# Attention into two MoE blocks: the third turning moved to a scores' bank, and a row tile's scaling moved behind the minimum passes

## The chip, the cores and the metric

The kernel runs on one core of a Trainium2 chip. The metric is the time of one execution on the device, in microseconds, as the median of repeated runs; lower is better.

## The reference

Three layers follow each other. S is 576 keys, D is 64, there are 4 batches of 8 heads, so 2304 tokens of 512 numbers behind attention.

```python
scores = scale * np.matmul(q, k.transpose(0, 1, 3, 2))
thresh = np.max(scores, axis=-1, keepdims=True) - tau
scores = np.where(scores >= thresh, scores, -1000000000.0)
attn = np.exp(scores - np.max(scores, axis=-1, keepdims=True))
attn = attn / (np.sum(attn, axis=-1, keepdims=True) + 1e-09)
x = np.matmul(attn, v)                      # turned to [2304, 512]
...
noisy_logits = x @ w_gate + np.log1p(np.exp(x @ w_noise)) * noise
top2 = np.argpartition(-noisy_logits, 2, axis=1)[:, :2]
...
h = np.maximum(x[mask] @ w1[e], 0.0)        # for each of 8 experts, 512 -> 1024
out[mask] += top2_w[mask, k, None] * (h @ w2[e])
...
h = x @ w_in                                # 512 -> 2048
out = (np.maximum(h, 0.0) + alpha * np.minimum(h, 0.0)) @ w_out
```

## The kernel before

**Precision.** Every large matmul is done as three products of split operands: a high part, cast by ScalarE, and a low part, which POOL or VectorE makes as the difference of the number and its high part. L306 and L308 cast the high parts of q and k (`split_hi`), L316 on POOL makes the low parts (`split_lo`); L171 and L177 do the same for expert weights (`w_hi`, `w_lo`), L206 and L207 for expert rows.

**Units of attention.** Attention is cut in 80 units (`NU`): a batch, a block of 128 queries and a pair of heads; the last 64 queries of a batch make a tail unit ("t") that holds both heads in one block. Four units give one tile of 128 tokens. A unit passes these stages, each in an iteration of its own of the loop at L737:

- `s_mm` (L364): 12 matmuls make the scores, one allocation of `psum_s` per head. There are two such allocations, of two banks each; of a bank's 512 columns 288 are used.
- `d1` (L375, VectorE): a pass over the scores of one head that copies them out and finds the row's extreme value; it frees the banks. Called the minimum pass here, since the sign is turned.
- `a1` (L386, ScalarE): the exponential. `thresh` (L380, ScalarE): the threshold.
- `d2` (L399, VectorE): masks the exponentials below the threshold and sums them, called the masking pass.
- `t_mm` (L416, L418, L420, TensorE): turns the masked probabilities by 128x128 blocks, in parts of 4, 4 and 1 blocks, called the first, second and third turning, each into a bank of `psum_t`, of which there are three. `a2` (L428, L430, L432, ScalarE) copies each part out.
- `pv` (L449 to L454): the products with V, in the one allocation of `psum_v`; `group_evac` (L470, L475, L477, ScalarE) copies a finished tile out.

Iteration i works on unit i+1's scores, unit i's minimum, exponential and threshold, unit i-1's masking, unit i-2's turnings (`DT` = 2) and unit i-3's products.

**Stages of a tile.** When a tile is out, `x_stages` spreads its later steps over the next iterations: `rows` (L488 and L489 invert the sums; L498 turns the tile, L500 on VectorE scales it, L502 stores it), `logits` (L508, copied by L511 on ScalarE), `flip` (L515 turns the logits), `sum_` (L519, L522 on VectorE). `gating` then computes noisy logits, top-2 (L570 to L577, VectorE), ranks (L582 to L587, TensorE), places (L593 to L597) and sends the rows to the experts' lists (L617, L618, POOL) for groups of three tiles.

**What sets the order.** The order is written by hand: on each engine instructions run in the order in which the program issues them, and buffers are handed out in rings. A table `at` holds extra steps by iteration and slot; before, slot 0 lies behind the next unit's scores and ahead of `pv`, slot 1 at the iteration's end. An instruction that uses a PSUM bank waits for whoever used that bank before it.

**Expert 0.** Its first 256 rows don't depend on gating's result. From iteration 66 on its weights are loaded and split, in iterations 78 and 79 its two row tiles are turned (L203 in `x_split`, in a `psum_t` bank) and split, and from iteration 80 on `do_fill` puts one piece of its products (L214 first, then L232) into each iteration. Behind the loop the other experts and the last layer follow.

## Time and profile before

| | us |
|---|---|
| median of 3 runs | 1167.44 |
| lowest and highest run | 1166.29, 1167.62 |
| the profiled execution's own time | 1170.81 |
| its span | 1169.1 |

| engine | busy us | share of the span |
|---|---|---|
| TensorE, matmuls (PE) | 1135.2 | 97% |
| TensorE, weight loads (PEld) | 977.5 | 84% |
| VectorE (DVE) | 622.8 | 53% |
| ScalarE (ACT) | 532.0 | 46% |
| GpSimd (POOL) | 532.8 | 46% |

The mean granted clock of TensorE is 0.997 of full speed. A row of the timeline gives start and length in us, engine, line, operation and tiles, how many instructions it joins and, in brackets, how long the engine was idle ahead of it and whose end it waited for. Attention runs from the start to about 320 us, the experts and the last layer fill the rest.

### The profile page before, as it was taken

What the parts mean: (1) busy time and instruction counts of PE and PEld (TensorE: products, weight loads), DVE (VectorE), ACT (ScalarE), POOL (GpSimd) and SP (SyncE); (2) the same over time, 40 slices, a digit from 0 to 9 for tenths busy, and PEclk for the clock granted to TensorE, in tenths of its full rate; (3) what the DMA queues carried; (4) which work ended last, traced back from release to release, by engine and by line L of the source; (5) the groups of instructions that cost most, each with busy time, mean ns of one, the idle gap of its engine ahead of it and who ended that gap; (6) DMA issues with size and microseconds to landing.
All of it is one profiled execution on the core that took longest, in us unless ns stands there. A gap on an engine that the chain in (4) does not pass through costs nothing. (4 is left out here: it accounts for less than half of the span.)

```text
span 1169.1 us, 20453 instructions
## 1 busy us (share of the span) xinstructions
PE 1135.2 (97%) x7754; PEld 977.5 (84%) x7754; DVE 622.8 (53%) x1332; ACT 532.0 (46%) x1039; POOL 532.8 (46%) x632
## 2 busy tenths in 40 slices
PE   7999989999899999999999999999999999999997
PEld 6887777877789999999989898998888888888886
DVE  7978788899644544454545453445443343342221
ACT  7977768788624544444444454433211211211111
POOL 7636534654524545455454555556332333332221
PEclk9999999999999999999999999999999999999999
DMA  7423222132357676567667565541321321320001
GB/s 219 137 86 122 92 77 74 73 119 92 136 141 207 184 199 194 183 171 213 192 189 202 186 188 190 166 151 54 86 66 25 92 66 27 90 64 10 36 1 39
DMA packets 156552, 141.50 MB, mean 121 GB/s; under 512 B 108576, under 2 KB 109216, under 8 KB 156448
## 3 DMA queue, kind: packets, MB, share of 16 engines
q1 hardware_dynamic: 150400, 120.91, 35.1%
q0 software_dynamic: 5760, 18.88, 4.8%
q8 instruction: 63, 1.03, 0.4%
q14 instruction: 41, 0.34, 0.1%
q10 hardware_dynamic: 288, 0.34, 0.1%
HBM read 97.11 MB, written 42.99 MB: 120 GB/s over the span
## 5 line engine op out<-in xcount | busy, mean ns | idle before, releaser
L214 PE MATMUL ps_t<-m_v,m_pair 128*128 128x384 f32 (+2 forms) x1216 | 220.0, 317 | 0.3 <-DVE m_v L207 0.3
L177 POOL TENSOR_TENSOR m_pair<-m_v,m_pair 128x512 fp32r<-128x512 f32 x114 | 151.9, 1353 | 130.0 <-ACT m_pair L171 106.7
L214 PEld LDWEIGHTS ps_t<-m_v,m_pair 128*128 128x128 f32 x1216 | 186.8, 190 | 8.1 <-DVE m_v L207 0.5
L232 PE MATMUL ps_s<-m_pair,m_hh 128*128 128x512 f32 x528 | 167.5, 390 | 0.0
L995 DVE TENSOR_SCALAR m_tmp<-ps_t,alpha_t 128x512 f32<-128x512 f32 (+1 forms) x80 | 55.7, 697 | 208.6 <-PE ps_t L214 200.9
L225 DVE SCALAR_TENSOR_TENSOR m_gate<-ps_t,m_hh 128x384 fp32r<-128x384 f32 (+1 forms) x120 | 58.8, 493 | 169.9 <-ACT m_hh L224 169.8
L399 DVE SCALAR_TENSOR_TENSOR m_hh<-m_tmp,sm,m_hh 128x576 f32<-128x576 f32 x144 | 126.1, 908 | 2.4 <-ACT sm L380 2.0
L214 PE MATMUL ps_t<-m_v,m_early 128*128 128x256 f32 (+2 forms) x672 | 127.3, 320 | 0.0
L232 PEld LDWEIGHTS ps_s<-m_pair,m_hh 128*128 128x128 f32 x528 | 99.1, 188 | 20.3
L1000 POOL TENSOR_TENSOR m_v<-m_tmp,m_v 128x512 fp32r<-128x512 f32 x39 | 50.4, 1293 | 139.7 <-ACT m_v L999 139.7
L375 DVE TENSOR_SCALAR_CACHE_REDUCE m_tmp<-ps_s 128x576 f32<-128x576 f32 x144 | 103.6, 752 | 18.5 <-PE ps_s L364 16.0
L386 ACT ACTIVATE m_hh<-m_tmp,sm 128x576 f32<-128x576 f32 x144 | 105.7, 783 | 11.0 <-DVE m_tmp L375 10.9
L214 PEld LDWEIGHTS ps_t<-m_v,m_early 128*128 128x128 f32 x672 | 105.9, 189 | 5.1 <-DVE m_v L207 0.4
L364 PE MATMUL ps_s<-m_pair 64*128 64x288 f32 (+1 forms) x864 | 95.3, 318 | 12.9 <-DVE m_tmp L375 8.3
L999 ACT CAST m_v<-m_tmp 128x512 fp32r<-128x512 f32 x39 | 24.2, 620 | 173.5 <-DVE m_tmp L996 173.5
L232 PE MATMUL ps_s<-m_pair,m_gate 128*128 128x512 f32 x264 | 102.9, 390 | 0.0
L224 ACT ACTIVATE m_hh<-ps_t 128x384 fp32r<-128x384 f32 (+1 forms) x120 | 52.7, 439 | 98.3 <-PE ps_t L214 96.8
L1000 POOL TENSOR_TENSOR m_gate<-m_tmp,m_gate 128x512 fp32r<-128x512 f32 (+1 forms) x41 | 44.1, 1077 | 116.1 <-ACT m_gate L999 109.9
L364 PEld LDWEIGHTS ps_s<-m_pair 64*128 64x128 f32 (+1 forms) x864 | 72.3, 191 | 28.1 <-DVE m_tmp L375 14.3
L1019 PE MATMUL ps_s<-m_pair,m_v 128*128 128x512 f32 x396 | 95.1, 389 | 0.0
L1019 PE MATMUL ps_s<-m_pair,m_gate 128*128 128x512 f32 x360 | 88.3, 391 | 0.0
L1019 PEld LDWEIGHTS ps_s<-m_pair,m_v 128*128 128x128 f32 x396 | 74.3, 188 | 15.4
(229 smaller groups left out, 1982.0 us busy)
## 6 DMA issues: line engine op xcount, KB each, us to landing
m_v<-in_w_dram SPq DMA_DIRECT2D x64, 512.0 KB
yg<-m_tmp SPq DMA_DIRECT2D x40, 256.0 KB
m_tmp<-in_w_in_dram SPq DMA_DIRECT2D x16, 512.0 KB
m_tmp<-in_w_out_dram SPq DMA_DIRECT2D x16, 512.0 KB
m_early<-in_kt_dram SPq DMA_DIRECT2D x15, 320.0 KB
yg<-m_gate SPq DMA_DIRECT2D x18, 256.0 KB
m_rows<-xg SPq DMA_DIRECT2D x72, 64.0 KB
out_dram<-m_tmp SPq DMA_DIRECT2D x18, 256.0 KB
```

The source lines that it names most:

```text
L177: eng.tensor_tensor(WL[n][:, w], raw[:, w], f32(WH[n][:, w]), op=OP.subtract)
L214: pe.matmul(ps[:, :n], w[wc[d]][:, col:col + 128], x[xx][:, d, :n], start=(k == 0), stop=(k == 11))
L224: act.activation(h, ps, AF.Relu)
L225: dve.scalar_tensor_tensor(hs[1][:, f * n:f * n + n], ps, 0.0, f32(h), op0=OP.max, op1=OP.subtract)
L232: pe.matmul(ps, a[:, o:o + 128], ww[w][:, c:c + 512], start=(f == 0 and k == 0), stop=(f == nf - 1 and k == 2))
L364: pe.matmul(u["ps", h][:, x, :288], lhs, kk[r, o:o + 288], start=(k == 0), stop=(k == 2))
L375: dve.tensor_scalar(u["sp"][:, h].rearrange("p (a b) -> p a b", a=2), ps[:, :, :288], -0.125, None, op0=OP.mult, op1=OP.min, accum_out=u[" ...
L386: act.activation(u["em"][:, h], u["sp"][:, h], AF.Exp, bias=u["sm"][:, h:h + 1], scale=-1.0)
L399: dve.scalar_tensor_tensor(u["em"][:, h], u["sp"][:, h], sm[:, 2 + h:3 + h], u["em"][:, h], op0=OP.is_le, op1=OP.mult, accum_out=acc)
L995: dve.tensor_scalar(g, ps, 0.0, alpha_t[:, f:f + 1], op0=OP.min, op1=OP.mult)
L1000: pool.tensor_tensor(h[:, n:2 * n], g, f32(h[:, :n]), op=OP.subtract)
L1019: pe.matmul(ps, h[x][:, t * 128:t * 128 + 128], ww[w][:, c:c + 512], start=(f == 0 and k == 0), stop=(f == 15 and k == 2))
```

## The change

The third turning of a unit no longer takes a bank of `psum_t`. `s_bank` allocates the next unit's score banks ahead of the turnings, and the third turning writes into columns 384 to 511 of the last of these banks, which the scores leave free; only for the last three units it stays in `psum_t`. ScalarE's copy of it comes behind the threshold and behind the scores in program order. A new slot -1 lies behind the exponentials of unit i and ahead of the masking passes of unit i-1; the scaling of a tile (`scale_rows`), the copy and the sum of its logits, top-2 and the places go there, while the matmuls for them stay at an iteration's end. `split_hi` and `w_hi` go from slot 1 to slot 0. Expert 0's two row tiles are turned in iteration 79 into two score allocations, and split in iteration 80 behind the last `w_hi`. Two pieces of its first product share one allocation.

```diff
--- before.py
+++ after.py
@@ -201,6 +201,9 @@
             else:
                 for c in range(HP):
                     pe.transpose(ps[:, c * 128:c * 128 + 128], src[:, c * 128:c * 128 + 128], ident)
+            x_halves(ps, j, x)
+
+        def x_halves(ps, j, x):
             pv_ = ps.rearrange("p (c t) -> p c t", c=HP)
             xh = x[0][:, :, j * 128:j * 128 + 128]
             act.copy(xh, pv_)
@@ -351,8 +354,6 @@
             b, c, hp = units[i]
             qh, ql, kh, kl, zh, zl = sets[b * HP + hp]
             u = st[i]
-            for h in range(nh(i)):
-                u["ps", h] = psum_s()
             q0 = 0 if c == "t" else c * 128 + (64 if b % 2 else 0)
             for x in range(2):
                 for k, (q, z, kk) in enumerate(((qh, zh, kh), (qh, zh, kl), (ql, zl, kh))):
@@ -365,6 +366,10 @@
 
         def nh(i):
             return 1 if units[i][1] == "t" else 2
+
+        def s_bank(i):
+            for h in range(nh(i)):
+                st[i]["ps", h] = psum_s()
 
         def d1(i, h):
             u = st[i]
@@ -408,7 +413,7 @@
             u = st[i]
             em = u["em"]
             emf = em.rearrange("p h s -> p (h s)")
-            ps = psum_t()
+            ps = psum_t() if part < 2 or i + DT + 1 >= NU else st[i + DT + 1]["ps", nh(i + DT + 1) - 1][:, 1, 384:]
             u["pt", part] = ps
             if part < 2:
                 o = part * 640
@@ -488,27 +493,41 @@
                 dve.tensor_scalar(e, e, 1e-9, None, op0=OP.add)
                 dve.reciprocal(e, e)
 
-            def rows():
+            def turn_rows():
                 x = xts[T]
+                g["rows"] = psum_t()
+                for c in range(HP):
+                    pe.transpose(g["rows"][:, c * 128:c * 128 + 128], x[:, c], ident)
+
+            def scale_rows():
                 e = esum[T]
                 if "inverse" not in g:
                     inverse()
-                ps = psum_t()
-                for c in range(HP):
-                    pe.transpose(ps[:, c * 128:c * 128 + 128], x[:, c], ident)
+                ps = g["rows"]
                 xtok[T] = xtok_ring()
                 dve.tensor_tensor(xtok[T].rearrange("p (h d) -> p h d", h=H), ps.rearrange("p (h d) -> p h d", h=H),
                                   e[:, :, None].to_broadcast([128, H, D]), op=OP.mult)
                 sp.dma_start(xd[T * 128:T * 128 + 128], xtok[T])
 
+            def rows():
+                turn_rows()
+                scale_rows()
+
             def logits():
+                logits_mm()
+                logits_copy()
+
+            def logits_mm():
                 x = xts[T]
                 ps = psum_t()
+                g["lp"] = ps
                 for c in range(HP):
                     pe.matmul(ps[c * 32:c * 32 + 32, :128], wcat[:, c], x[:, c], start=True, stop=True,
                               skip_group_check=True)
+
+            def logits_copy():
                 g["lt"] = lt_ring()
-                act.copy(g["lt"], ps[:, :128])
+                act.copy(g["lt"], g["lp"][:, :128])
 
             def flip():
                 g["ps"] = psum_t()
@@ -521,6 +540,9 @@
                                   esum[T][:, :, None].to_broadcast([128, H, 16]), op=OP.mult)
                 dve.tensor_reduce(lg[:, T], t.rearrange("p (h j) -> p j h", h=H), axis=AX.X, op=OP.add)
 
+            if T < NT - 2:
+                return [(0, 1, turn_rows), (1, -1, scale_rows), (1, 1, logits_mm), (2, -1, logits_copy),
+                        (2, 1, flip), (3, -1, sum_)]
             return [(0, 1, rows), (1, 1, logits), (2, 1, flip), (3, 0, sum_), (0, 0, inverse)]
 
         def bc8(ap, n):
@@ -622,12 +644,12 @@
             sends = [(T, k) for T in range(t0, t1) for k in range(2)]
             first = [exp_, one_plus, log_, noisy, top2]
             if 3 < t1 <= 12:
-                plan = [(d, 1, f) for d, f in enumerate(first)] + [(5, 1, rank), (6, 0, place)]
+                plan = [(d, 1, f) for d, f in enumerate(first[:4])] + [(5, -1, top2), (5, 1, rank), (6, -1, place)]
                 if t1 == FIRST:
                     plan.append((9, 0, close))
                 return plan + [(6 + q, 1, lambda a=a: send(*a)) for q, a in enumerate(sends)]
             if t1 <= 15:
-                plan = [(d // 2, 1, f) for d, f in enumerate(first)] + [(4, 1, rank), (5, 0, place)]
+                plan = [(d // 2, 1, f) for d, f in enumerate(first[:4])] + [(3, -1, top2), (4, 1, rank), (5, -1, place)]
                 return plan + [(5 + q // 2, 1, lambda a=a: send(*a)) for q, a in enumerate(sends)]
             if t1 == NT:
 
@@ -683,7 +705,7 @@
             next_load()
 
         for i, n, p, eng in sched:
-            put(i, split_hi, n, p)
+            put((i, 0) if i > 8 else i, split_hi, n, p)
             put(i + 1, do_lo, n, p, eng)
 
         def zero_init(e):
@@ -700,17 +722,28 @@
         put(64, w_load, 1)
         for n in range(W0):
             i = 66 + 2 * n
-            put(i, w_hi, n)
+            put((i, 0), w_hi, n)
             put(i + 1, w_lo, n, pool)
             put(i + 1, w_load, n + 2)
+        x0_bank = {}
+
+        def x0_turn(t):
+            x0_bank[t] = psum_s()[:, 0]
+            src = xrows.pop((0, t))
+            for c in range(HP):
+                pe.transpose(x0_bank[t][:, c * 128:c * 128 + 128], src[:, c * 128:c * 128 + 128], ident)
+
         for t in range(BLOCK0 // 128):
             put(70, x_load, 0, t)
-            put(NU - 4 + DT + t, lambda t: x_split(xrows.pop((0, t)), t, X0, psum_t, False), t)
+            put(NU - 1, x0_turn, t)
+            put((NU, 0), lambda t: x_halves(x0_bank[t], t, X0), t)
 
         fill = []
 
         def first_1(f):
-            ps = psum_s()[:, f % 2]
+            if f % 2 == 0:
+                g2["up"] = psum_s()
+            ps = g2["up"][:, f % 2]
             relu(f, BLOCK0, mm1(ps, BLOCK0, [0, 1, 2, 3], X0, f * 128), H0)
 
         g2 = {}
@@ -734,6 +767,7 @@
                 f(*a)
 
         END = NU + DT + 1
+        s_bank(0)
         s_mm(0)
         for i in range(END):
             it, iv = i - DT, i - DT - 1
@@ -746,19 +780,24 @@
                     d1(i, h)
                 for h in range(nh(i)):
                     a1(i, h)
+            for f, a in at.pop((i, -1), []):
+                f(*a)
             if 0 < i <= NU:
                 for h in range(nh(i - 1)):
                     d2(i - 1, h)
             if tiles and nh(it) == 2:
                 t_mm(it, 1)
                 a2(it, 1)
+            if i + 1 < NU:
+                s_bank(i + 1)
             if tiles:
                 t_mm(it, 2)
-                a2(it, 2)
             if i < NU:
                 thresh(i)
             if i + 1 < NU:
                 s_mm(i + 1)
+            if tiles:
+                a2(it, 2)
             for f, a in at.pop((i, 0), []):
                 f(*a)
             if i == END - 1:
@@ -772,8 +811,6 @@
                         if T == NT - 1:
                             last_rows.append(todo[0][2])
                             todo = [(i + 1, 0, todo[1][2]), (i + 1, 0, todo[4][2]), (i + 2, 0, todo[2][2]), (i + 2, 0, todo[3][2])]
-                        else:
-                            todo = todo[:4]
                         if T == NT - 2:
                             todo = [(i + d, p, f[2]) for (d, p), f in zip(((1, 1), (1, 1), (2, 1), (2, 1)), todo)]
                         for t0, t1 in GROUPS:
```

VectorE around the rows of a tile, before (L375 the minimum passes, L399 the masking passes, L488 and L489 the inverse, L500 the scaling of the turned rows; `x2` is two instructions):

```order
L375 TENSOR_SCALAR m_tmp,sm_152<-ps_s 128x576 [waits PE_49] x2
L399 SCALAR_TENSOR_TENSOR m_hh,es_147<-m_tmp,sm_151,m_hh 128x576 [waits Activation_49]
L399 SCALAR_TENSOR_TENSOR m_hh,es_147<-m_tmp,sm_151,m_hh 128x576
L519 TENSOR_TENSOR m_rows<-ps_t,es_145 128x128 [waits PE_49]
L522 TENSOR_REDUCE m_rows<-m_rows 128x16 [waits DVE_49]
L488 TENSOR_SCALAR es_146<-es_146 128x8
L489 RECIPROCAL es_146<-es_146 128x8 [waits DVE_49]
L500 TENSOR_TENSOR m_gate<-ps_t,es_146 128x512 [waits DMAHW3_49,DMAHW2_49,DMAHW4_49,DMAHW1_49,DMAHW5_49,DMAHW0_49,DMAHW7_49,DVE_49,PE_49]
L375 TENSOR_SCALAR m_tmp,sm_153<-ps_s 128x576 x2
L399 SCALAR_TENSOR_TENSOR m_hh,es_142<-m_tmp,sm_152,m_hh 128x576 [waits Activation_49]
L399 SCALAR_TENSOR_TENSOR m_hh,es_142<-m_tmp,sm_152,m_hh 128x576
```

The same place of the change (L380 the minimum passes, L404 the masking passes, L493, L494 and L508 as L488, L489 and L500 before):

```order
L538 TENSOR_TENSOR m_rows<-ps_t,es_145 128x128 [waits PE_49]
L541 TENSOR_REDUCE m_rows<-m_rows 128x16 [waits DVE_49]
L404 SCALAR_TENSOR_TENSOR m_hh,es_147<-m_tmp,sm_151,m_hh 128x576 x2
L380 TENSOR_SCALAR m_tmp,sm_153<-ps_s 128x576 [waits DVE_49,PE_49]
L380 TENSOR_SCALAR m_tmp,sm_153<-ps_s 128x576 [waits DVE_49,Activation_49]
L493 TENSOR_SCALAR es_146<-es_146 128x8
L494 RECIPROCAL es_146<-es_146 128x8 [waits DVE_49]
L508 TENSOR_TENSOR m_gate<-ps_t,es_146 128x512 [waits DMAHW3_49,DMAHW2_49,DMAHW4_49,DMAHW1_49,DMAHW5_49,DMAHW0_49,DMAHW7_49,DVE_49,PE_49]
L404 SCALAR_TENSOR_TENSOR m_hh,es_142<-m_tmp,sm_152,m_hh 128x576 x2
```

L519 and L522 (now L538 and L541) and the scaling went from behind the masking passes to a place ahead of them and behind the minimum passes; the second minimum pass waits for ScalarE.

ScalarE in three units of the same stretch, before (L428 and L430 the copies of the turnings, L386 the exponentials, L380 the threshold, L511 the copy of the logits, L308 a cast):

```order
L428 COPY m_tmp<-ps_t 128x512 [waits PE_49,Activation_49]
L386 ACTIVATE m_hh<-m_tmp,sm_148 128x576 [waits DVE_49] x2
L428 COPY m_tmp<-ps_t 128x512 [waits PE_49,Activation_49]
L430 COPY m_tmp<-ps_t 128x128 [waits PE_49,Activation_49]
L380 ACTIVATE sm_148<-sm_148,taut 128x2
L511 COPY m_rows<-ps_t 128x128 [waits PE_49]
L428 COPY m_last<-ps_t 128x512 [waits PE_49,Activation_49]
L386 ACTIVATE m_hh<-m_tmp,sm_149 128x576 [waits DVE_49] x2
L428 COPY m_last<-ps_t 128x512 [waits PE_49,Activation_49]
L430 COPY m_last<-ps_t 128x128 [waits PE_49]
L380 ACTIVATE sm_149<-sm_149,taut 128x2
L308 CAST m_pair<-m_early 128x640 [waits DMAHW3_49]
```

The same place of the change (L433 and L435 the copies, L391, L385, L530 and L311 as L386, L380, L511 and L308):

```order
L433 COPY m_tmp<-ps_t 128x512 [waits PE_49,Activation_49]
L391 ACTIVATE m_hh<-m_tmp,sm_148 128x576 [waits DVE_49] x2
L433 COPY m_tmp<-ps_t 128x512 [waits PE_49,Activation_49]
L385 ACTIVATE sm_148<-sm_148,taut 128x2
L435 COPY m_tmp<-ps_s 128x128 [waits PE_49,Activation_49]
L433 COPY m_last<-ps_t 128x512 [waits PE_49,Activation_49]
L391 ACTIVATE m_hh<-m_tmp,sm_149 128x576 [waits DVE_49] x2
L530 COPY m_rows<-ps_t 128x128
L433 COPY m_last<-ps_t 128x512 [waits PE_49,Activation_49]
L385 ACTIVATE sm_149<-sm_149,taut 128x2
L435 COPY m_last<-ps_s 128x128 [waits PE_49,Activation_49]
L311 CAST m_pair<-m_early 128x640 [waits DMAHW3_49]
```

The copy of the third turning reads `ps_s` and stands behind the threshold, the copy of the logits behind the exponentials.

TensorE ahead of expert 0's first product, before (L418 the third turning, L452 and L454 the products with V of units 76 and 77, L203 an expert row tile, L498 and L508 rows and logits of a tile, L214 the product):

```order
L203 MATMUL ps_t<-ident,m_v_73 128x128 [waits DMAHW4_49,Activation_49]
L203 MATMUL ps_t<-ident,m_v_73 128x128 x3
L498 MATMUL ps_t<-ident,m_last 128x128 [waits Activation_49]
L498 MATMUL ps_t<-ident,m_last 128x128 x3
...
L416 MATMUL ps_t<-ident,m_hh 128x128 x3
L418 MATMUL ps_t<-ident,m_hh 128x128 [waits Activation_49]
L452 MATMUL ps_v<-m_last,m_v_74 64x128 x8
L454 MATMUL ps_v<-m_last,m_v_74 64x128 x2
L214 MATMUL ps_s<-m_pair,m_early 128x256 x2
L214 MATMUL ps_s<-m_pair,m_early 128x256 [waits Pool_49]
```

The same place of the change (L423, L457, L459, L734, L500, L525 and L217 for them):

```order
L734 MATMUL ps_s<-ident,m_v_73 128x128 [waits DMAHW3_49]
L734 MATMUL ps_s<-ident,m_v_73 128x128 x3
L734 MATMUL ps_s<-ident,m_v_73 128x128 [waits DMAHW4_49]
L734 MATMUL ps_s<-ident,m_v_73 128x128 x3
L500 MATMUL ps_t<-ident,m_last 128x128 [waits Activation_49]
...
L421 MATMUL ps_t<-ident,m_hh 128x128 x3
L423 MATMUL ps_t<-ident,m_hh 128x128 [waits DVE_49]
L457 MATMUL ps_v<-m_last,m_v_74 64x128 x8
L459 MATMUL ps_v<-m_last,m_v_74 64x128 x2
L217 MATMUL ps_s<-m_pair,m_early 128x256 [waits DVE_49,Activation_49]
L217 MATMUL ps_s<-m_pair,m_early 128x256 [waits DVE_49]
```

Both row tiles are turned in one go into `ps_s` banks, and expert 0's first product waits for ScalarE and VectorE, who split them.

## Rows read from the trace of the kernel before

**Rows 1.** Busy time by stretch of the program, all engines.

```profile
core 0: us, PE busy (x) PEld busy (x) DVE busy (x) ACT busy (x) POOL busy (x), PEclk, DMA share, GB/s
17.40:81.90 64.50, 64.38 (x779) 54.95 (x778) 55.56 (x145) 57.66 (x139) 36.03 (x61) 1.00 0.41 126
81.90:217.00 135.10, 123.67 (x1435) 99.43 (x1433) 112.94 (x337) 102.92 (x228) 67.51 (x122) 0.99 0.27 91
...
252.20:299.70 47.50, 43.27 (x496) 34.59 (x494) 45.33 (x116) 39.27 (x82) 23.10 (x25) 1.00 0.34 112
299.70:341.00 41.30, 36.29 (x327) 31.25 (x327) 19.48 (x78) 16.79 (x41) 18.48 (x31) 1.00 0.37 136
341.00:1150.00 809.00, 808.72 (x4166) 709.30 (x4165) 348.19 (x543) 274.98 (x462) 351.17 (x284) 1.00 0.44 126
```

**Rows 2.** Waits of weight loads, 81.9 to 217 us: sum us, times, longest us.

```profile
PEld ps_s L364 <- DVE m_tmp L375: 8.1, 19, 0.5
PEld ps_t L418 <- ACT m_tmp L428: 5.6, 8, 1.9
```

**Rows 3.** Waits of VectorE in the same stretch.

```profile
DVE m_gate L500 <- PE ps_t L498: 10.3, 8, 1.9
...
DVE m_gate L500 <- DMA xg<-m_gate,posi: 3.1, 1, 3.1
```

**Rows 4.** Timeline of an undisturbed unit, 44.4 to 48.1 us, single instructions.

```profile
44.47 0.62 ACT L428 COPY m_last<-ps_t 128x512 f32<-128x512 f32 x1
...
44.69 1.05 PE L364 MATMUL ps_s<-m_pair 64*128 64x288 f32 x12
...
46.29 0.61 ACT L428 COPY m_last<-ps_t 128x512 f32<-128x512 f32 x1
...
46.76 0.31 ACT L430 COPY m_last<-ps_t 128x128 f32<-128x128 f32 x1
46.91 0.35 ACT L380 ACTIVATE sm<-sm,taut 128x2 f32<-128x2 f32 x1
...
47.11 0.30 ACT L470 COPY m_last<-ps_v 128x128 f32<-128x128 f32 x1
...
48.05 0.40 PE L364 MATMUL ps_s<-m_pair 64*128 64x288 f32 x2
```

**Rows 5.** Timeline of a disturbed tile, 187 to 197 us.

```profile
187.43 0.69 DVE L500 TENSOR_TENSOR m_gate<-ps_t,es 128x512 f32<-128x512 f32 x1 [1.73 <-PE ps_t L498]
...
188.71 0.75 DVE L375 TENSOR_SCALAR_CACHE_REDUCE m_tmp<-ps_s 128x576 f32<-128x576 f32 x1
...
189.53 1.05 PE L364 MATMUL ps_s<-m_pair 64*128 64x288 f32 x11 [0.28 <-DVE m_tmp L375]
...
195.69 0.81 DVE L399 SCALAR_TENSOR_TENSOR m_hh<-m_tmp,sm,m_hh 128x576 f32<-128x576 f32 x1
196.26 2.32 POOL L316 TENSOR_TENSOR m_pair<-m_early,m_pair 128x320 fp32r<-128x320 f32 x2 [3.06 <-ACT m_pair L308]
...
196.43 1.41 DVE L399 SCALAR_TENSOR_TENSOR m_hh<-m_tmp,sm,m_hh 128x576 f32<-128x576 f32 x1
```

**Rows 6.** Groups of VectorE's instructions by line and form, 81.9 to 217 us.

```profile
L399 DVE SCALAR_TENSOR_TENSOR m_hh<-m_tmp,sm,m_hh 128x576 f32<-128x576 f32 x63 | 53.1, 877 | 0.5 <-ACT sm L380 0.5
```

**Rows 7.** Timeline of attention's end, 302 to 309 us.

```profile
302.53 1.05 ACT L171 CAST m_pair<-m_v 128x1024 fp32r<-128x1024 f32 x1
...
303.48 0.59 ACT L206 CAST m_pair<-ps_t 128x512 fp32r<-128x512 f32 x1
...
304.61 0.66 PE L416 MATMUL ps_t<-ident,m_hh 128*128 128x128 f32 x4 [1.42 <-ACT m_last L428]
...
305.30 1.09 PE L452 MATMUL ps_v<-m_tmp,m_v 128*64 128x128 f32 x16
...
307.47 0.66 PE L203 MATMUL ps_t<-ident,m_v 128*128 128x128 f32 x4 [0.86 <-ACT m_last L428]
...
308.79 0.69 DVE L207 TENSOR_TENSOR m_pair<-ps_t,m_pair 128x512 fp32r<-128x512 f32 x1 [0.81 <-ACT m_pair L206]
```

## The prediction

> **What bounds the kernel now.** I read the table of busy times by stretch first, then the waits of the most stalled stretch, then single instructions of one undisturbed and one disturbed unit, and the end of attention last.
>
> The table [rows 1] shows where TensorE has idle time at all. From 341 us on its matmul column is busy for 808.72 of 809.00 us. So whatever is saved before that point moves the end by as much, one to one, and nothing behind it is touched by the change. From 17.4 to 81.9 us it is full too (64.38 of 64.50). The idle time lies between: 11.4 us from 81.9 to 217, 4.2 us from 252.2 to 299.7, 5.0 us from 299.7 to 341. These are attention's 128-token tiles with the stages of x and of gating mixed in, and the hand-over to expert 0.
>
> In the stretch of 135.1 us, TensorE's weight loads wait for two things [rows 2]: 8.1 us in 19 waits for VectorE's minimum pass of the scores (L375, which frees the scores' banks) and 5.6 us in 8 waits for ScalarE's copies of the turned probabilities (L428, which free the turning banks). VectorE in turn waits 10.3 us in 8 waits for the turning of a tile's rows, L498, before it can scale them in L500, and once 3.1 us for a DMA [rows 3]. Eight waits are one per tile. That is a ring: L500 stands ahead of the minimum passes in VectorE's order, its input is turned by TensorE behind the products with V, and TensorE's next scores stand behind the minimum passes. One turn of it [rows 5]: L500 starts at 187.43 after 1.73 us of idle time, the second minimum pass only at 188.71, and the eleven remaining score matmuls at 189.53, 0.82 us behind its start.
>
> An undisturbed unit [rows 4] takes 3.36 us (scores at 44.69 and 48.05), and there ScalarE runs without a gap: the copy of the first turning at 44.47, of the second at 46.29, of the third at 46.76, threshold at 46.91, evacuation at 47.11.
>
> **The change part by part. The slot behind the exponentials.** The same L488, L489 and L500, the same L519 and L522, and the top-2 work of gating now stand behind both minimum passes of unit i and ahead of the masking passes (L399) of unit i-1, and the turned rows have been on TensorE for the length of the minimum passes. Nothing is added on VectorE. The 10.3 us of waits for L498 leave the path of the scores. What is late next is the masking, which TensorE's next turning needs; it has the slack of about a unit. With ScalarE's copy of the logits behind the exponentials, and two instead of three turning banks taken per unit, the 5.6 us behind L428 should go as well.
>
> What can be won in the stretch from 81.9 to 217 has to be bounded, since no row shows it without stalls. One bound is the matmul column's idle time, 11.4 us. The other is the share of the weight loads: 54.95 of 64.50, or 85.2%, in the full stretch, and 99.43 of 135.10, or 73.6%, here. At 85.2% the same loads would take 99.43 / 0.852 = 116.7 us, 18.4 less. The profile says of the matmul column that its ends are modelled, so I start from 116.7. I add what stays: the masking pass takes 0.877 us on average here [rows 6] and up to 1.41 [rows 5] where POOL subtracts beside it (63 of them, so 0.07 x 63 = 4.2 us over the 0.81 of a free one [rows 5], of which I put 3 on the path); three top-2 steps ahead of masking, an estimate of 2 us; the DMA wait of L500 [rows 3], which now holds up masking alone, 1 us of its 3.1. That is 122.7, so **12.4 us saved**, kept between 5 and 18.4.
>
> The Trainium skill, "Perfetto Trace Analysis", section "Identifying the Most-Contended Engine", says that matmul busy time is a poor measure of headroom because matmuls are pipelined, and that the share of weight loads is the better one. By the matmul column the saving here would end at 11.4 us, by the rule at 18.4; the 12.4 that I take is already over the first, so the result tests the rule.
>
> From 252.2 to 299.7 VectorE is busy 45.33 of 47.50 us, so at most 2.2 us are to be had there, whatever TensorE's idle 4.2; I take **1.5 saved**.
>
> **The third turning in a scores' bank.** It costs no instruction, but it adds a wait. ScalarE's copy of it now stands behind the threshold, and VectorE's second minimum pass of the next unit reads the same bank, so it waits for that copy; before, no minimum pass waited for ScalarE. From the undisturbed unit [rows 4]: threshold where L430 was, 46.76; copy 0.20 later (46.91 to 47.11), 46.96; its 0.31 us end at 47.27; then the minimum pass, and the scores 0.82 us behind it, 48.09, against 48.05 without the new wait. So the slack is nil where ScalarE has a cast in each unit, and about 0.15 where it has none. In the full stretch from 17.4 to 81.9 (19 units of 3.36 us) I charge 0.05 each: **1.0 lost**. In the stalled stretch ScalarE is busy 102.92 of 135.10 us and its copy comes in time by more than the others need. The copy also has to wait for the unit's last score matmul, which ends in the same bank; that is at 44.69 + 1.05 = 45.74 [rows 4], over a microsecond ahead of the copy, so it costs nothing until the scores themselves are that late.
>
> **Casts ahead of the evacuation.** The L306 and L308 casts, and expert 0's L171, swap places with L470 or L477 on ScalarE, between 0.30 us (L470, [rows 4]) and 1.05 us (L171, [rows 7]) either way. POOL's subtractions start that much earlier, the products' bank is free that much later; TensorE needs that bank a unit later. Nothing, covered by that unit.
>
> **Expert 0's rows.** Before, the two turnings L203 sit in the turning banks: TensorE waits 1.42 us at 304.61 for a copy queued behind L171 and L206, and 0.86 at 307.47 [rows 7]. Both go, 2.3 us. In their place, L171 for the last weight block (0.95 from its start to the next), two L206 (0.59 each) and one L207 (0.69) now stand between ScalarE's last copy of unit 78 and expert 0's first product: 2.8 us, with only the products with V (1.09 and a short rest) to cover it. That is a new wait of 1.5 to 2.0 us; I take 1.7. Net **0.6 saved**. That two blocks share an allocation of scores' banks afterwards moves nothing: from there weight loads follow each other.
>
> Sum: -12.4 - 1.5 + 1.0 - 0.6 = -13.5 us. The profiled execution took 1170.81 us and would go to 1157.3; it lies 3.4 above the median of the three runs, so against that median the forecast is 1167.4 - 13.5 = **1153.9 us**.
>
> **The rivals.** First, VectorE or POOL takes over as the bound. VectorE is busy 112.94 of 135.10 us, and with the extra work ahead of masking, masking can be late for the next turning. For it: the pass of 1.41 us beside POOL's subtraction (2.32 us for two) at 196.26 [rows 5]. The Trainium skill, "SBUF — State Buffer", section "Who interferes with whom", says that a VectorE instruction with two SBUF inputs and a GpSimd instruction that reads SBUF exclude each other; that row agrees. Against it: the full stretch has the same pairs without a stall. Half of the 12.4 would then be lost: -13.5 + 6.2 = -7.3 us, 1160.
>
> Second, everything goes as the weight loads' share says: 18.4 + 2.2 + 2.3 - 1.7 with no loss early, 21.2 saved, 1146.
>
> Third, on the other side: the new link. A copy that is late on ScalarE now stops the minimum pass, and so the scores. ScalarE has casts, evacuations, logit copies and gating steps in some units. About 60 units have the link. It decides from 14.5 / 60 = 0.24 us per unit (14.5 being the sum without the 1.0); at 0.35, a little over one L470 [rows 4], it costs 21 and leaves +6.5, 1174 us. Against it: ScalarE is idle for 32 of the 135 us of the stalled stretch [rows 1].
>
> That the change does not do what it says can be left out: the order shows the third turning going to a scores' bank and the scaling behind the minimum passes.
>
> **How the numbers follow.** A measurement of this kernel tells about 0.2%, 2.3 us, from no change. Forecast 0.58, VectorE or POOL as the bound 0.20, all of it 0.09, the link 0.13. Of the link's 0.13 about 0.04 lies within 0.2% and 0.08 above, of the first rival 0.02 within and 0.01 above. That makes faster 0.85, no change 0.06, slower 0.09. The range reaches from 1145, just past the second rival's 1146, to 1165, past the first one's 1160 by the 5 us that a smaller gain in the stalled stretch would take, and leaves the link out.
>
> **What would show it.** Right: VectorE's wait for the turned rows under 3 us instead of 10.3; no L428 group over 1 us in the weight loads' waits; the stretch of 8 tiles about 123 us long, with weight loads near 81%; a wait of 1.5 to 2 us ahead of expert 0's first product; the early units at 3.36 to 3.45 us. Wrong: minimum passes that wait for the copy of the third turning by more than 0.2 us in most units (the link), or turnings that wait for the masking pass (the first rival).

## The result and the profile after

| | before | after |
|---|---|---|
| median, us | 1167.53 (6 runs) | 1157.11 (6 runs) |
| lowest and highest | 1166.29, 1168.70 | 1156.42, 1157.99 |
| ratio, 95% interval | | 0.9915 [0.9904, 0.9925] |
| profiled execution, span | 1170.81, 1169.1 | 1157.01, 1155.2 |

The change makes the kernel 10.4 us faster; the forecast was 13.5 (1153.9 us, range 1145 to 1165). The lines of the kernel move with the change: L364 becomes L365 (scores), L375 L380 (minimum pass), L399 L404 (masking), L500 L508 (scaling), L416 and L418 L421 and L423 (turnings), L428 and L430 L433 and L435 (their copies), L206 and L207 L209 and L210, L214 and L225 L217 and L228 (expert 0's first product and VectorE's pass over it).

Busy time by stretch in the profile after, columns as in [rows 1]; the second row holds the same eight tiles as 81.9 to 217 us before, the fourth the hand-over to expert 0:

```profile
17.40:83.30 65.90, 64.58 (x779) 54.89 (x778) 59.85 (x146) 57.60 (x139) 36.78 (x61) 1.00 0.40 123
81.90:204.30 122.40, 117.04 (x1450) 96.87 (x1446) 116.25 (x339) 102.09 (x232) 65.03 (x123) 1.00 0.30 100
240.00:285.00 45.00, 41.80 (x492) 33.68 (x492) 43.76 (x116) 38.24 (x83) 22.79 (x25) 1.00 0.34 118
285.00:326.00 41.00, 36.21 (x324) 30.87 (x325) 21.16 (x78) 16.10 (x40) 19.42 (x31) 1.00 0.36 134
326.00:1135.00 809.00, 808.57 (x4164) 708.69 (x4163) 348.38 (x541) 275.58 (x462) 350.79 (x284) 1.00 0.44 126
```

The eight tiles take 122.4 us where they took 135.1 [rows 1]. VectorE is now busy 116.25 of these 122.4 us, so little is left there. The borders of the fourth row are round times set by hand, so its 41.0 us against 41.3 before say nothing of the hand-over's length; the table further down does.

Part of the 135.1 us is a fall of TensorE's granted clock, behind the DMA wait of [rows 3]. Windows of 2 us of the profile before (the clock is the third number from the end):

```profile
120.00:122.00 2.00, 1.72 (x14) 1.23 (x16) 2.00 (x7) 2.00 (x5) 1.73 (x3) 0.82 0.88 261
122.00:124.00 2.00, 2.00 (x20) 1.75 (x18) 2.00 (x6) 0.17 (x1) 1.25 (x3) 0.50 0.78 313
124.00:126.00 2.00, 2.00 (x21) 1.37 (x21) 0.84 (x4) 0.85 (x3) 0.00 (x0) 0.82 0.32 131
```

Reckoned as (1 - 0.82) + (1 - 0.50) + (1 - 0.82), times 2 us, it cost 1.7 us. The profile after has no such fall ahead of 1150 us, so of the 12.7 us saved here 1.7 are the clock's and 11.0 the rest.

The waits of the weight loads and of VectorE from 83.3 to 204.3 us (sum us, times, longest us) answer to [rows 2, 3]:

```profile
PEld ps_s L365 <- DVE m_tmp L380: 6.1, 15, 0.5
...
PEld ps_t L421 <- DVE m_gate L615: 2.6, 3, 0.9
```

```profile
DVE m_tmp L380 <- ACT m_last L435: 3.1, 8, 0.7
...
DVE m_gate L508 <- DVE es L494: 0.2, 1, 0.2
```

The scaling waits for the turned rows no more (10.3 us before), and no group of waits for L433 is above 0.5 us (5.6 before for L428). What is new is VectorE's wait for ScalarE's copy of the third turning, 3.1 us; the prediction named this wait, but took it for nothing in this stretch.

Where the time went in the two profiles is read from the starts of the products with V of the same unit:

| from unit to unit | before | after | difference |
|---|---|---|---|
| start to 20 | 83.97 | 84.3 | +0.3 (it was +1.4 at unit 16) |
| 20 to 52 | 133.97 | 120.9 | -13.1 |
| 52 to 64 | 35.8 | 35.8 | 0.0 |
| 64 to 75 | 46.95 | 45.0 | -2.0 |
| 75 to the end of the span | 868.4 | 869.2 | +0.8 |

The last border is unit 75, since the wait of 1.42 us at 304.61 [rows 7], the first of the hand-over before, lies between the products of unit 75 and those of unit 76. Unit 75's start before, then after:

```profile
300.69 1.09 PE L452 MATMUL ps_v<-m_last,m_v 128*64 128x128 f32 x16
```

```profile
285.99 1.09 PE L457 MATMUL ps_v<-m_last,m_v 128*64 128x128 f32 x16
```

### The profile page after: what moved, and what is told of

It is laid out like the page before. It is cut to its first block, busy times and chain, and to the rows that moved or that the text cites. A ratio compares the mean times of both kernels' runs of the same rounds, so it can differ in the third digit from the quotient of the medians.

```text
span 1155.2 us, 20571 instructions
## 1 busy us (share of the span) xinstructions
PE 1127.1 (98%) x7754; PEld 972.9 (84%) x7754; DVE 631.7 (55%) x1332; ACT 529.4 (46%) x1039; POOL 531.3 (46%) x632
## 5 line engine op out<-in xcount | busy, mean ns | idle before, releaser
L217 PE MATMUL ps_t<-m_v,m_pair 128*128 128x384 f32 (+2 forms) x1216 | 220.4, 317 | 0.4 <-DVE m_v L210 0.3
L217 PEld LDWEIGHTS ps_t<-m_v,m_pair 128*128 128x128 f32 x1216 | 186.8, 190 | 8.9 <-ACT m_v L209 0.6
L228 DVE SCALAR_TENSOR_TENSOR m_gate<-ps_t,m_hh 128x384 fp32r<-128x384 f32 (+1 forms) x120 | 58.7, 492 | 167.9 <-ACT m_hh L227 167.8
L404 DVE SCALAR_TENSOR_TENSOR m_hh<-m_tmp,sm,m_hh 128x576 f32<-128x576 f32 x144 | 131.6, 946 | 0.0
L217 PE MATMUL ps_t<-m_v,m_early 128*128 128x256 f32 (+2 forms) x672 | 127.2, 320 | 0.0
L380 DVE TENSOR_SCALAR_CACHE_REDUCE m_tmp<-ps_s 128x576 f32<-128x576 f32 x144 | 104.8, 751 | 19.8 <-ACT m_last L435 6.6
L217 PEld LDWEIGHTS ps_t<-m_v,m_early 128*128 128x128 f32 x672 | 105.8, 189 | 5.0 <-DVE m_v L210 0.3
L391 ACT ACTIVATE m_hh<-m_tmp,sm 128x576 f32<-128x576 f32 x144 | 105.2, 777 | 3.8 <-DVE m_tmp L380 3.7
L365 PE MATMUL ps_s<-m_pair 64*128 64x288 f32 (+1 forms) x864 | 88.3, 316 | 12.9 <-DVE m_tmp L380 7.8
L365 PEld LDWEIGHTS ps_s<-m_pair 64*128 64x128 f32 (+1 forms) x864 | 68.7, 191 | 26.6 <-DVE m_tmp L380 16.8
```

The source lines that it names most:

```text
L217: pe.matmul(ps[:, :n], w[wc[d]][:, col:col + 128], x[xx][:, d, :n], start=(k == 0), stop=(k == 11))
L228: dve.scalar_tensor_tensor(hs[1][:, f * n:f * n + n], ps, 0.0, f32(h), op0=OP.max, op1=OP.subtract)
L365: pe.matmul(u["ps", h][:, x, :288], lhs, kk[r, o:o + 288], start=(k == 0), stop=(k == 2))
L380: dve.tensor_scalar(u["sp"][:, h].rearrange("p (a b) -> p a b", a=2), ps[:, :, :288], -0.125, None, op0=OP.mult, op1=OP.min, accum_out=u[" ...
L391: act.activation(u["em"][:, h], u["sp"][:, h], AF.Exp, bias=u["sm"][:, h:h + 1], scale=-1.0)
L404: dve.scalar_tensor_tensor(u["em"][:, h], u["sp"][:, h], sm[:, 2 + h:3 + h], u["em"][:, h], op0=OP.is_le, op1=OP.mult, accum_out=acc)
```

## The experiments

The runs were made in three groups, each on one chip beside the kernel before, whose median there was 1170.0 to 1170.6 us and not 1167.5; ratios are to the kernel before on the same chip. They stand as recorded and differ from the quotients of the medians by up to 0.001. The changed kernel itself, run as e0_changed in the second group, has 0.9926 [0.9912, 0.9939], just above the 0.9925 expected of it.

**The scaling's place alone, and the third turning's place alone.** e2_slot keeps the third turning in the scores' bank and undoes the slot:

```diff
-            if T < NT - 2:
-                return [(0, 1, turn_rows), (1, -1, scale_rows), (1, 1, logits_mm), (2, -1, logits_copy),
-                        (2, 1, flip), (3, -1, sum_)]
+            if T < NT - 2:
+                return [(0, 1, rows), (1, 1, logits), (2, 1, flip), (3, 0, sum_)]
...
-                plan = [(d, 1, f) for d, f in enumerate(first[:4])] + [(5, -1, top2), (5, 1, rank), (6, -1, place)]
+                plan = [(d, 1, f) for d, f in enumerate(first)] + [(5, 1, rank), (6, 0, place)]
...
-                plan = [(d // 2, 1, f) for d, f in enumerate(first[:4])] + [(3, -1, top2), (4, 1, rank), (5, -1, place)]
+                plan = [(d // 2, 1, f) for d, f in enumerate(first)] + [(4, 1, rank), (5, 0, place)]
```

> The change with one part undone: scaling, sum of logits, top-2, places and the copy of the logits stand where they stood before the change; the third turning stays in the scores' bank. Ring theory (the gain comes from taking the scaling out of the ring between VectorE's minimum passes and TensorE's scores): most of the gain goes, 1164 to 1168, with some 8 waits of VectorE for the turned rows of over 1 us again. Banks theory (the gain comes from the freed turning bank): 1157 to 1160, the waits for turned rows shorter than before.

Measured: 1183.59 us, ratio 1.0109 [1.0094, 1.0123], slower than the kernel before. e3_third keeps the slot and gives the third turning its bank of `psum_t` back:

```diff
-            ps = psum_t() if part < 2 or i + DT + 1 >= NU else st[i + DT + 1]["ps", nh(i + DT + 1) - 1][:, 1, 384:]
+            ps = psum_t()
...
                 t_mm(it, 2)
+                a2(it, 2)
             if i < NU:
                 thresh(i)
...
-            if tiles:
-                a2(it, 2)
```

> The change with one part undone: the third turning takes a bank of psum_t again, and its copy stands ahead of the threshold. Ring theory: little is lost, 1157 to 1160, and VectorE's waits for that copy (9.8 us in sum from 17 to 204 us) are gone. Banks theory: 1164 to 1168, with TensorE's waits of over 1 us for the copies of turned probabilities back. If the new link is a net burden (the third rival of the prediction, in small): 1154 to 1156.

Measured: 1171.03 us, ratio 0.9999 [0.9987, 1.0010]: no gain. Each theory is refuted as the only cause. The weight loads' waits of e2_slot, 82 to 205 us:

```profile
PEld ps_s L365 <- DVE m_tmp L380: 9.4, 17, 1.2
PEld ps_s L423 <- DVE m_tmp L380: 5.5, 7, 1.7
PEld ps_s L423 <- PE ps_t L421: 4.4, 5, 0.9
```

and of e3_third in the same stretch:

```profile
PEld ps_t L423 <- DVE m_gate L508: 7.7, 7, 2.8
```

With the scaling still ahead of the minimum passes, a third turning in the scores' bank waits for these passes too, and so for the scaling: it has joined the ring, with 5.5 us of waits for VectorE. With the scaling moved behind them, the bank of `psum_t` that holds the turned rows is held longer, and a third turning that needs one of the three banks waits for the scaling, 7.7 us in 7 waits; the ring has only changed its link. So the two edits are one: the scaling may come later only because the third turning has left the banks that it holds. Part of both times is a second price: windows of 2 us show six falls of the granted clock to 0.50 in the profile of e2_slot and five in that of e3_third, worth 10.2 and 10.3 us (reckoned as above). Without them the spans would be 1172.8 and 1164.4 us, 1159.0 for e0_changed and 1166.6 for the kernel before (e11_before). So at full clock the slot alone might win some 2 us, and the freed bank alone still loses; these are single profiles, taken on different chips.

**The casts.** e1_casts puts ScalarE's casts of q and k behind the evacuation again:

```diff
-            put((i, 0) if i > 8 else i, split_hi, n, p)
+            put(i, split_hi, n, p)
```

> The change with one part undone: ScalarE's casts of q and k stand behind the evacuation again. In the changed kernel the stretch from 17.4 us to the 20th unit takes 1.4 us longer than before, and masking passes between 40 and 73 us take 1.20 us on average (before: 0.945). Theory A (POOL's subtractions start earlier and fall on the masking passes): masking back near 0.95 us there, the early stretch back to within 0.5 us of before, the time 1155.5 to 1156.3. Theory B (the early loss is the new wait of the minimum pass for ScalarE's copy of the third turning): masking may get shorter, but the early stretch keeps at least 1 us of its loss, time 1156.8 to 1158.

Masking passes from 40 to 73 us (count, then busy us and mean ns), before, after, and in e1_casts:

```profile
L399 DVE SCALAR_TENSOR_TENSOR m_hh<-m_tmp,sm,m_hh 128x576 f32<-128x576 f32 x17 | 15.6, 945 | 1.4 <-ACT sm L380 1.3
```

```profile
L404 DVE SCALAR_TENSOR_TENSOR m_hh<-m_tmp,sm,m_hh 128x576 f32<-128x576 f32 x17 | 19.9, 1198 | 0.0
```

```profile
L404 DVE SCALAR_TENSOR_TENSOR m_hh<-m_tmp,sm,m_hh 128x576 f32<-128x576 f32 x17 | 15.5, 940 | 0.0
```

With the casts undone the passes are short again, and unit 16 starts 0.1 us before its time in the kernel before instead of 1.4 behind. VectorE's waits for ScalarE's copies in this stretch rose meanwhile, from 5.6 us in the changed kernel to 8.5. So theory A holds for the place: the early loss needs the earlier casts, with which POOL's subtractions fall on masking passes, and it is not the new wait by itself. But the casts alone don't make it either. e3_third keeps them and takes only the third turning out of the scores' bank; its passes are short too:

```profile
L404 DVE SCALAR_TENSOR_TENSOR m_hh<-m_tmp,sm,m_hh 128x576 f32<-128x576 f32 x17 | 15.6, 945 | 1.2 <-ACT sm L385 1.1
```

Its unit 16 starts 0.5 us behind the first profile of the kernel before and level with the second; e2_slot, which has both edits, has passes of 1188 ns and starts it 1.3 and 0.9 us behind these. So it takes both edits together to bring subtractions and masking passes onto each other. In the whole time (1161.56 us, 0.9927 [0.9914, 0.9939]) the gain of e1_casts doesn't show against 0.9926 of the changed kernel, and the time that theory A named did not come; the runs of both spread over 4 us, for a reason given below.

**The casts of expert 0's weights**, moved back as well, on top of three edits (e7_all, below):

```diff
-            put((i, 0), w_hi, n)
+            put(i, w_hi, n)
```

> e7_all with expert 0's weight casts behind the evacuation as well, as in the kernel before, so the casts' move is undone altogether. Theory A (casts ahead of the evacuation only move POOL's subtractions onto the masking passes, for weights as for q and k): 0.5 to 1.5 us less than e7_all. Theory B (in this stretch POOL's subtractions of 1.25 us fall on masking passes either way): within 0.5 us. If the early cast is what POOL waits for: 0.5 to 1.5 us more.

Measured: 1157.86 us, 0.9891 [0.9875, 0.9908]. By the ratios this is 1.4 us above e7_all (0.9879), which ran on another chip. That is the third case named, but the intervals overlap, so the sign is not shown. With both moves of the casts and the shared allocation undone, this kernel keeps only the slot, the third turning's place and the turning of expert 0's row tiles in scores' banks, and the gain is there.

**The hand-over.** e4_x0 undoes the whole part, e5_own the shared allocation alone (the second piece of this diff):

```diff
-            put(NU - 1, x0_turn, t)
-            put((NU, 0), lambda t: x_halves(x0_bank[t], t, X0), t)
+            put(NU - 4 + DT + t, lambda t: x_split(xrows.pop((0, t)), t, X0, psum_t, False), t)
...
-            if f % 2 == 0:
-                g2["up"] = psum_s()
-            ps = g2["up"][:, f % 2]
+            ps = psum_s()[:, f % 2]
```

> The change with one part undone: expert 0's row tiles are turned in the turning banks in iterations 78 and 79 and split at once, and each piece of its first product has an allocation of its own. By the two traces the change removed waits of 1.4 and 0.9 us there and added 1.8 ahead of the first product and 1.1 and 0.6 ahead of its fourth and sixth piece. Theory A (this part gives back what it wins): 1156 to 1158.5. Theory B (it is worth its 2.3 us): 1159 to 1160.5.

> The changed kernel itself, beside the next three on one chip, so that they can be compared with it. All theories: its ratio to the kernel before stays at 0.990 to 0.9925, a new profile shows the early stretch 1.2 to 1.6 us longer than before and the wait of 1.8 us ahead of expert 0's first product again.

> The change with one part undone: each piece of expert 0's first product takes an allocation of scores' banks of its own again. Theory A (inside a shared allocation the next piece waits for VectorE's pass over the piece before, although it lies in another bank, so two pieces are never in flight): the waits of 1.05 and 0.4 us ahead of the fourth and sixth piece go, 0.8 to 2 us less than the changed kernel. Theory B (the waits only move on to the last piece, which waits for VectorE in any case): within 0.5 us of the changed kernel.

Measured: e4_x0 1158.41 us, 0.9898 [0.9884, 0.9912]; e5_own 1159.35 us, 0.9906 [0.9891, 0.9922]; e0_changed 1163.13 us on e5_own's chip. At its ratio e4_x0 would be at 1155.6 us on the first chip, under both theories: the part takes back more than it wins. The profiles agree: from unit 75 to the end e4_x0 takes 867.1 us, the changed kernel 869.2 in its first profile and 872.0 in e0_changed, the kernel before 868.4. The shared allocation alone costs 3.8 us in the medians, more than theory A had for it. The waits ahead of expert 0's first product in the timeline after, then in e5_own:

```profile
296.18 0.35 PE L217 MATMUL ps_s<-m_pair,m_early 128*128 128x256 f32 x1 [1.56 <-DVE m_pair L210]
...
306.32 1.34 PE L217 MATMUL ps_s<-m_pair,m_early 128*128 128x256 f32 x9 [1.05 <-DVE m_pair L228]
...
311.02 1.34 PE L217 MATMUL ps_s<-m_pair,m_early 128*128 128x256 f32 x9 [0.39 <-DVE m_pair L228]
...
315.48 1.34 PE L217 MATMUL ps_s<-m_pair,m_early 128*128 128x256 f32 x9 [1.32 <-DVE m_pair L228]
```

```profile
299.85 1.72 PE L217 MATMUL ps_s<-m_pair,m_early 128*128 128x256 f32 x9 [1.56 <-ACT m_pair L209]
...
317.69 1.34 PE L217 MATMUL ps_s<-m_pair,m_early 128*128 128x256 f32 x9 [1.64 <-DVE m_pair L228]
```

The fourth piece starts at 306.32, when VectorE's pass over the third (305.85, 0.42 us long) ends, though it writes another bank of the allocation: the second piece of a pair waits for the first to be read, so what is tracked here is the allocation and not the bank. Two pieces in flight became one, and VectorE's pass stands behind gating's last steps. The profiles of e0_changed and e5_own are 5.5 us apart: 1.8 are these waits (1.05 and 0.39 in e0_changed alone, and 1.96 against 1.64 ahead of the last piece), 3.4 the granted clock. Windows of 2 us of e0_changed (columns as in [rows 1], the clock third from the end):

```profile
318.00:320.00 2.00, 1.83 (x16) 1.62 (x14) 1.82 (x9) 0.64 (x3) 1.78 (x4) 1.00 0.67 270
320.00:322.00 2.00, 0.22 (x1) 0.22 (x2) 1.13 (x5) 0.39 (x1) 0.00 (x0) 1.00 0.63 244
322.00:324.00 2.00, 2.00 (x16) 1.91 (x16) 0.00 (x0) 0.08 (x1) 0.00 (x0) 0.71 0.03 8
324.00:326.00 2.00, 2.00 (x5) 1.61 (x6) 0.75 (x4) 0.31 (x1) 0.67 (x1) 0.50 0.00 0
326.00:328.00 2.00, 2.00 (x11) 1.37 (x11) 0.62 (x4) 0.00 (x0) 1.35 (x3) 0.94 0.32 131
```

TensorE is busy 0.22 of 2 us ahead of the last piece; then the clock stands at 0.50, the lower of its two levels, for over 3 us. The same happens at 302 to 306 us, behind the wait ahead of the first piece. One such fall costs 1.7 us here ((1 - 0.71) + (1 - 0.50) + (1 - 0.94), times 2 us), as much as that in the profile before. In the profile after and in those of e4_x0, e5_own and e7_all there is none. Five runs of e0_changed show it by their mean clock: 1160.43 and 1160.73 us at 0.999 and 0.998, 1163.13, 1163.20 and 1164.24 at 0.996. This is the spread of 4 us.

**An earlier split of the row tiles.** e6_halves splits them behind their turning in iteration 79:

```diff
-            put((NU, 0), lambda t: x_halves(x0_bank[t], t, X0), t)
+            put((NU - 1, 2), lambda t: x_halves(x0_bank[t], t, X0), t)
...
             for f, a in at.pop((i, 1), []):
                 f(*a)
+            for f, a in at.pop((i, 2), []):
+                f(*a)
```

> The change with one step moved: expert 0's two row tiles are split at the end of iteration 79, right behind their turning, and no longer behind the last weight cast in iteration 80. Theory A (the cast and the splits ahead of the first product are what TensorE waits for): the wait of 1.8 us goes, 1.2 to 2 us less than the changed kernel. Theory B (the splits then delay ScalarE's next copies of turned probabilities, which TensorE needs first): within 0.5 us of the changed kernel.

Measured: 1160.95 us, 0.9920 [0.9906, 0.9933]. The wait ahead of the first piece is gone from the trace, and the median is 2.2 us below e0_changed. Theory A, with overlapping intervals. With the wait one of the two falls of the clock is gone as well, 1.7 us by itself, so how much of the 2.2 the wait alone is worth stays open.

**Three edits at once.** e7_all is the changed kernel with the edits of e1_casts, e5_own and e6_halves:

> The changed kernel with three edits at once: casts of q and k behind the evacuation as before, an allocation for each piece of expert 0's first product, row tiles split at the end of iteration 79. If the three losses are real and apart from each other: 1.4 + 1.3 + 1.6, so 3 to 5 us less than the changed kernel, the best of all. If they share one slack (VectorE or ScalarE at the hand-over): 1.5 to 2.5 us less.

Measured: 1156.24 us, 0.9879 [0.9864, 0.9894], 6.9 us below e0_changed on the same chip, more than the sum of the three losses, since the falls of the clock go too; its runs lie within 1.3 us. It beats both kernels.

**Two steps further.** e8_piece7 gives the last piece of expert 0's first product another bank, e10_copy has ScalarE's copy of the third turning ahead of the threshold, each on top of e7_all:

```diff
-            ps = psum_s()[:, f % 2]
+            ps = psum_v() if f == 7 else psum_s()[:, f % 2]
```

> The kernel with the three edits (e7_all), and the last piece of expert 0's first product in the products' bank psum_v, which is free by then. In e7_all this piece waits 1.9 us for VectorE's pass over the sixth. Theory A (that wait is for the bank alone): ratio to before 0.001 to 0.0015 lower than that of e7_all (0.9879), 1 to 1.7 us. Theory B (TensorE's next instructions, the ranks of the last rows, wait for the same VectorE work): no lower, within 0.0004.

```diff
             if tiles:
                 t_mm(it, 2)
-            if i < NU:
-                thresh(i)
             if i + 1 < NU:
                 s_mm(i + 1)
             if tiles:
                 a2(it, 2)
+            if i < NU:
+                thresh(i)
```

> e7_all with ScalarE's copy of the third turning ahead of the threshold. Link theory (the second minimum pass waits for this copy, 0.20 us earlier is 0.20 us won in each unit where it is last): 0.5 to 2 us less than e7_all, VectorE's waits for L435 and L437 (some 9 us from 82 to 310 us) nearly halved. Rival (the copies that VectorE waits for are late because ScalarE was late by whole microseconds in a few places): within 0.5 us, the largest waits of 2.0 and 1.3 us are still there.

Measured: e8_piece7 1155.64 us, 0.9870 [0.9853, 0.9886]; e10_copy 1155.84 us, 0.9873 [0.9857, 0.9890]. In e8_piece7 the last piece's wait is gone, but no more than 0.0009 of the ratio, less than theory A wanted and inside the interval. In e10_copy VectorE's largest waits for these copies stay (1.9 and 1.3 us), as the rival said. Neither can be told from e7_all.

**The kernel before once more.** e11_before is the kernel before, for a second profile.

> A second profile of the kernel before. In the profile that the prediction was read from, one wait of 3.1 us for a DMA ahead of L500 at 118 us was followed by a stretch at a granted clock of 0.5, and that execution lies 3.4 us above the median. Theory A (both are an accident of that execution): this profile has neither, and its 8 tiles take 130 to 133 us instead of 135.1. Theory B (they belong to the kernel): the wait is there again, 2.5 to 3.5 us.

Measured: 1171.74 us in one run; units 20 to 52 take 134.1 us, as in the first profile (134.0). At the place of the DMA wait of [rows 3] stands

```profile
118.37 0.69 DVE L500 TENSOR_TENSOR m_gate<-ps_t,es 128x512 f32<-128x512 f32 x1 [2.67 <-PE ps_t L498]
```

The wait is there again, put down to the turned rows this time: theory B for the wait. The falls of the clock lie elsewhere (162 to 168 and 258 to 264 us instead of 120 to 126), so the wait need not bring one: in this profile the clock stays at 1.00 from 118 to 126 us.

## Why the prediction was right, and where it was off

**What bounds the kernel** was read rightly. All that was won lies ahead of 326 us, and behind it the stretch of 809 us is as full as before.

**The eight tiles** were forecast at 122.7 us and took 122.4; the waits that were to go are gone. The weight loads stand at 96.87 of 122.40, 79%, near the 81% named. That the number came so close is in part luck. 1.7 of the 12.7 us are the fall of the clock, which the sum doesn't name, though [rows 1] has the clock of this stretch at 0.99. In the later profiles of e0_changed, e4_x0, e5_own and e6_halves, units 20 to 52 take 123.2 to 124.1 us instead of 120.9. And the term was booked on the slot behind the exponentials alone, with the freed bank as an addition. e3_third shows the slot without the freed bank at no gain, e2_slot the freed bank without the slot at a loss; the step "it costs no instruction, but it adds a wait" took the third turning for a cost, and without it there is no gain.

The test of the matmul column comes out less sharply than it looks. The 12.7 us saved are more than the column's 11.4 us of idle time, but without the fall of the clock it is 11.0, which is not. What speaks against the column as a measure is where the 11.0 us came from. After the change 5.4 us of its idle time are left (122.40 - 117.04), so an estimated 6.1 us came out of idle time and 4.9 out of busy time, with the same work. The Trainium skill, "Perfetto Trace Analysis", section "Identifying the Most-Contended Engine", says that matmul busy time is not a good measure, because pipelined matmuls look smaller in a trace, and names the share of the weight loads instead. The 4.9 us agree with the first half; the 18.4 us of headroom by the second were not reached, and VectorE, busy 116.25 of 122.40 us, leaves little room for them.

**The late tiles** were put at 1.5 us, at most 2.2 by VectorE's idle time; units 64 to 75 gave 2.0 in the two profiles.

**The early loss** of 1.0 us came out as 1.4 at unit 16 and 0.3 at unit 20, and by another mechanism. The step that failed is "Casts ahead of the evacuation ... Nothing": with the third turning in the scores' bank, the earlier casts bring POOL's subtractions onto the masking passes, 1198 instead of 945 ns. The loss is no 0.05 us in each unit: units 7 and 8 take 3.72 and 3.94 us, where 3.36 to 3.45 was named. The wait for ScalarE's copy, to which the loss was charged, rose in e1_casts while the loss went. This is the first rival's mechanism in small. The Trainium skill, "SBUF — State Buffer", section "Who interferes with whom", says that a VectorE instruction with two SBUF inputs contends with a GpSimd instruction that reads SBUF; the longer passes agree.

**The hand-over** is the step that failed in size and sign: 0.6 saved was forecast, and the two profiles show 0.8 lost from unit 75 to the end. The new wait ahead of the first piece was sized rightly (1.7 forecast, 1.56 on the matmuls, 1.8 on the weight loads). "That two blocks share an allocation of scores' banks afterwards moves nothing" is wrong: e5_own shows 3.8 us for it on its chip, in waits and in falls of the clock.

**The sum.** By the two profiles the change is worth 13.9 us against 13.5 forecast, but the errors cancel: 0.7 more saved in units 20 to 52, 0.5 in the late tiles, 0.7 less lost early, and 1.4 missed at the hand-over. The medians decide, and they are 10.4 us apart. The profile of before lies 3.3 us above its runs' median; its fall of the clock is 1.7 of them if those runs had none, which isn't on record.

**The other side**, the link, did not decide: VectorE waited for the copies of the third turning by 0.7 us at most from 83.3 to 204.3 us, and by 1.4 at most ahead of that.

## What to carry to other kernels

An edit that lengthens the life of a buffer and one that frees a buffer of the same ring must be priced together; here neither alone brought a gain that the runs show. Before two users share an allocation, look at what the dependence tracking works by: here a second bank of the same allocation is no second buffer. A cast that comes earlier brings the work of another engine forward with it, so look at what this work then falls on. Before a stretch is taken as the measure of a saving, look at its clock.

## What was not expected of the hardware

A wait of one to three microseconds on TensorE had a second price. Behind some of them the granted clock went to 0.50 for over 3 us, 1.7 us lost each time; the profiles of e2_slot and e3_third show six and five such falls in spans of 1183.0 and 1174.7 us, those of the kernel before one and two. The changed kernel has none in the first profile and two in e0_changed. Its gain may so differ from chip to chip, 0.9915 where it was first timed and 0.9926 there, but the intervals overlap.

One thing stays open. In e0_changed ScalarE's copy of a first turning starts late and puts down no reason that fits:

```profile
154.60 0.59 ACT L433 COPY m_last<-ps_t 128x512 f32<-128x512 f32 x1 [4.08 <-PE ps_s L365]
```

Its turning ended some two microseconds earlier, and the scores named as the releaser are not its input. It costs some 2 us at unit 39 (5.43 us from unit 38's products to unit 39's, against 3.47 in the first profile after). e1_casts and e4_x0 to e10_copy have the same long unit there.
